# Pooled attention with a two-layer network on one core: the first pair's start in another order, last stores from two engines, query pooling and bound transposes at other places of a pair's fourth step

## The chip, the cores and the metric

One Trainium2 chip, one core. The metric is the device time of one execution in microseconds (us). The kernel before took 812.07 us (median of three runs, 811.73 to 814.13). The engines are named as the profile names them: PE is TensorE (PEld its weight loads), DVE is VectorE, ACT is ScalarE, POOL is GpSimd, SP is SyncE, which here only issues transfers.

## The reference, cut to what matters

```python
# q, k, v: (4, 8, 1152, 64) float32;  batch, heads, rows, head width
q_pool = q.reshape(B, H, S // 2, 2, D).mean(axis=3)
scores = scale * np.matmul(q_pool, k.transpose(0, 1, 3, 2))
attn = np.exp(scores - scores.max(-1)); attn /= attn.sum(-1) + 1e-9
x = np.matmul(attn, v)                        # -> (4, 576, 512), all heads side by side
xn = (x - mean(x)) / np.sqrt(var(x) + 1e-6) * g_ln
out = x + np.maximum(xn @ w_ch1, 0) @ w_ch2   # w_ch1 (512, 2048), w_ch2 (2048, 512)
```

## The kernel before, in words

Two heads of one batch make a *pair*; there are 16 pairs, four to a batch. A pair has 576 pooled query rows per head, cut into 9 tiles of 128 rows (the fifth tile holds 64 rows of each head). One tile is one *step*, so there are 144 steps, and step `i` belongs to pair `i // 9` and has place `j = i % 9` in it. About 20 more steps finish the network. `step(i)` writes out the program; every engine runs its own instructions in just the order in which `step` emits them.

A step's own work: `emit_s` multiplies queries with keys (PE, L372 and L380) into three of the eight banks of `psum`, slot `i % 2`; `emit_max` copies the scores out and finds each row's largest (DVE, L392, "the search" below); `emit_exp` exponentiates (ACT, L399); `emit_hi` and `emit_lo` split the result into two 16-bit halves (ACT L410; DVE L419, or POOL L239 and L417 at places 2, 5 and 8), a transfer transposes them (SP, L422), and four steps later `emit_pv` multiplies with the values (PE, L462) into columns 128 to 257 of the last bank of the slot that holds the next step's scores. In the first 36 steps (batch 0, `on_pe`) TensorE transposes instead (L429) and `emit_pv` works in 32 bits (L453). In those steps the weights are also loaded and split.

From step 36 on each step also runs a *unit* of the two-layer network of a finished batch: 24 matmuls of the first layer (L613), whose result ACT and DVE split into `ht` (L626, L627), or 8 or 12 matmuls of the second (L645), whose end DVE adds into the output (L659).

Operands are scaled by powers of two taken from bounds. For pair `p`, during the steps of pair `p - 1` (queries in part a pair earlier): transfers bring keys and values (`load`, L117, L118, L121) and queries (`load_q`, L129); DVE or POOL adds the two rows that are pooled (`pool_q`, L162), POOL copies the sum (`dup_q`, L166); ACT sums absolute values into `acc` (`bound`, L182). At place 3 `scales_reduce` queues two pieces in `reds`: the first transposes `acc` on PE (L197), after which DVE takes the maximum and writes it on a diagonal (L200 `mx`, L201 `diag`); the second, one step later, multiplies the diagonal with ones on PE (L208), after which `scales` turns the exponent into factors (DVE, L231 `e`, L232 `s`, L234 `sc`). `place()` puts the results of L197 and L208 into columns 258 to 386 of that same last bank. `PREPS` lists the transposes of keys and queries (PE L285, L289, L312, L321) and their splits (ACT L274, L299; DVE L271, L294) at places 4 to 9.

What is read out of `psum` for a step is collected in `evacs` by `until(...)` and written out by `flush()` in the following step, after that step's search, in the order in which it was collected. `bank()` hands out a free bank for a unit or a prep.

Before step 0 the program loads the first tensors, keeps PE running with matmuls on the identity (`warm`, L1048), and goes through bounds, scales, transposes, splits and the first scores of pair 0 one after the other (L1070 to L1100).

Of the kernel before, what the change touches and what calls it, by code (L numbers as in the profile page):

```python
# [24 lines left out]
def tile_pooled_attention_moe(  # L25
# [198 lines left out]
    def scales(p, top, a=0, b=3):  # L224

        st = pair[p]
        e, s, sc = (st[x] for x in ("e", "s", "sc"))
        v = nc.vector
        ei, si = (x.bitcast(I32)[:, a:b] for x in (e, s))
        ti = top.bitcast(I32)  # L230
        v.tensor_scalar(ei, ti, EXPO, None, op0=ALU.bitwise_and)  # L231
        v.tensor_scalar(si, ti, EXPO, EXPO, op0=ALU.bitwise_and, op1=ALU.bitwise_xor)  # L232
        if a == 0:
            v.scalar_tensor_tensor(  # L234
                sc[:, 0:1], e[:, 0:1], -(2.0 ** -6), e[:, 1:2], op0=ALU.mult, op1=ALU.mult
            )
# [69 lines left out]
    def prep_q(p, u):  # L306

        qr, qt, s = raws[p, "q"], qt_of(p), pair[p]["s"]
        ps = bank()
        z = p % HP // 2  # L310
        if u == 2:
            nc.tensor.transpose(ps[:, 0:128], qr[:, C - 1].rearrange("p r d -> p (r d)"), ident)  # L312
            o, n = 512, 128
            hi, lo = (qt[:, a, o:o + n] for a in range(2))
            return split_from((p, "q", u), ps[:, 0:n], s[:, 1:2], hi, lo)

        d = (256, 128)[z]
        rows = ps.rearrange("p (a h n) -> p a h n", h=2, n=d)
        for c in range(4):
            a, n = (0, 64 * c) if z == 0 else (c // 2, 64 * (c % 2))  # L320
            nc.tensor.matmul(  # L321
                out=rows[:, a, :, n:n + 64], lhsT=qr[:, 4 * u + c].rearrange("p r d -> p (r d)"),
                rhs=ident.rearrange("p (h n) -> p h n", h=2), is_transpose=True, start=True, stop=True,
            )
        if z == 0:

            ps = ps.rearrange("p (h n) -> p h n", h=2)
            hi, lo = (
                pair[p]["qt+"][:, 1152 * a:1152 * a + 1280].rearrange("p (h n) -> p h n", h=2)[
                    :, :, 256 * u:256 * u + 256  # L330
                ]
                for a in range(2)
            )
        else:
            hi, lo = (qt[:, a, 640 * u:640 * u + 512] for a in range(2))
        return split_from((p, "q", u), ps, s[:, 1:2], hi, lo)

    PREPS = (
        ((prep_k, 0), (prep_k, 2), (prep_q, 0), (prep_q, 1), (prep_k, 1), (prep_q, 2)),
# [6 lines left out]
    def on_pe(i):  # L346

        return 0 <= i < HP * C
# [248 lines left out]
    def half_of(w, xn, xs, stores, fine=False):  # L597
# [36 lines left out]
        def l2(t, m0, m1):  # L634
# [22 lines left out]
            def evac():  # L657
                x = xs[t]
                nc.vector.scalar_tensor_tensor(  # L659
                    x, ps, inv12[:, w:w + 1], x, op0=ALU.mult, op1=ALU.add  # L660
                )
                if w == 1:
                    for o, dst in stores[t]:
                        nc.sync.dma_start(out=dst, in_=x[o:o + 64])
                    if len(xs) > 1:
                        room["x"] += 1
            return (evac,)
# [135 lines left out]
    for p in range(1, NP):  # L803
# [4 lines left out]
        if p == 1:  # L808
            pre(0, behind_scales)
            pre(i0 + 1, pool_q, p, nc.gpsimd)  # L810
            at(i0 + 1, dup_q, p, nc.gpsimd)
            at(i0 + 2, bound, p, "q")
        elif on_pe(i0):
            at(i0 - 4, load_q, p, (nc.sync,))
            at(i0 - 1, lambda p=p: calm.appendleft((lambda n: pool_q(p, nc.gpsimd), 0)))
            at(i0, lambda p=p: calm.appendleft((lambda n: dup_q(p, nc.gpsimd), 0)))
            at(i0 + 2, bound, p, "q")
        else:
            at(i0 - 8, load_q, p, (nc.sync,))
            at(i0 - 4, pool_q, p, nc.vector)  # L820
            at(i0 - 2, bound, p, "q")
            at(i0 - 1, dup_q, p, nc.gpsimd)
        if not on_pe(p * C):
# [140 lines left out]
    def step(i):  # L964
# [50 lines left out]
        if on_pe(i):  # L1015
            emit_t(i)
            if reds:
                found.append(reds.popleft()())
        elif reds:
            red = reds.popleft()  # L1020
            put = [None]
            until([lambda: put[0]()])
        while turned:
            n, ot = turned.popleft()
            emit_turn(n, ot, i)
        if not on_pe(i):
            if not first:
                a_piece(i)
            if red:
                put[0] = red()  # L1030
            if i in turns:
                a_prep()
            some_units(i)
            if i not in turns:
                a_prep()
        for fn, a in todo.pop(i, ()):
# [13 lines left out]
    with tc.manual_schedule():  # L1050
# [16 lines left out]
        nc.scalar.activation(out=wexp[:, 0:1], in_=nhalf, func=ACTF.Exp)  # L1067
        make_identity(nc, ident)

        warm(110)  # L1070
        st = state(0)
        nc.vector.memset(st["acc"], 0.0)
        pool_q(0, nc.vector)
# [10 lines left out]
            apply_absolute_value=True,  # L1084
        )
        nc.vector.tensor_tensor(st["acc"][:, 0:1], st["acc"][:, 0:1], st["acc"][:, 2:3], op=ALU.max)
        one, two = all_max(st["acc"][:, 0:2], 2, lambda ps: scales(0, ps, 0, 2))
        one()()
        two()()
        free_banks[:] = [6, 7, 3, 4]  # L1090
        parts = [fn(0, u) for fn, u in PREPS[0][:3]]
        for hi, lo in parts:
            hi()
            lo()
        warm(16)
        emit_s(0)
        preps.extend((fn, 0, u) for fn, u in PREPS[0][3:])
        free_banks[:] = [6, 7]
        for h in range(2):
# [34 lines left out]
```

## Time and profile before

| | |
|---|---|
| median of three runs | 812.07 us (811.73 to 814.13) |
| the profiled execution | 812.92 us, of it a span of 811.1 us from the first to the last instruction |
| busy: PE, DVE, ACT, POOL | 783.1, 599.3, 544.4, 341.3 us |
| share of the span on the chain that ended last | PE 67%, POOL 13%, DVE 10%, ACT 3% |

The profile gives for each instruction its start and duration and, where its engine stood idle before it, for how long and what ended the idle time. An engine's idle time costs something only where it is on the chain that ends last; here PE stands idle for only 28 us of 811, so the reading goes by stages and by PE's idle places.

### The profile page before, as it was taken

The page shows a single profiled execution, that of the slowest core. Times are in us where ns is not written, and L with a number is a line of the kernel's source. Part 1 is how long each engine was busy: PE and PEld are TensorE (multiplying, and loading weights), DVE is VectorE, ACT ScalarE, POOL GpSimd, SP SyncE. Part 2 cuts the span into 40 slices and gives each one's busy share as a digit, 9 for nine tenths or more (in the row PEclk, how much of TensorE's full clock was granted, in tenths as well). Part 3 has the DMA queues.
Part 4 walks back from the last instruction along what each step waited for, and adds up shares of the span by engine and source line. Part 5 has one row for each costly group of instructions (what it writes and reads, how often), then busy time and mean ns, then how long its engine had stood idle before and what let it go on. Part 6 is the DMA issues. An engine that isn't in the chain of part 4 may idle for free.

```text
span 811.1 us, 21365 instructions
## 1 busy us (share of the span) xinstructions
PE 783.1 (97%) x8978; PEld 553.7 (68%) x8978; DVE 599.3 (74%) x1174; ACT 544.4 (67%) x788; POOL 341.3 (42%) x338
## 2 busy tenths in 40 slices
PE   8899999989989999989999999999999999999997
PEld 7688888767556666657566666766675757766764
DVE  4599999999989887898777878888787867522121
ACT  3799898877786878787767776787778676211100
POOL 2010243389999963475452524528252423200000
PEclk9999999999999999999999999999999999999999
DMA  5828464208699999998998989896979687401001
GB/s 146 248 68 286 155 195 142 81 17 157 124 192 158 186 162 206 175 191 156 207 167 180 178 176 172 164 198 116 223 136 209 128 146 123 81 1 27 14 1 27
DMA packets 276017, 115.95 MB, mean 143 GB/s; under 512 B 259280, under 2 KB 259280, under 8 KB 275920
## 3 DMA queue, kind: packets, MB, share of 16 engines
q1 hardware_dynamic: 275840, 114.29, 69.9%
q8 instruction: 70, 1.15, 0.6%
q10 hardware_dynamic: 80, 0.29, 0.2%
q14 instruction: 27, 0.22, 0.1%
HBM read 46.14 MB, written 4.72 MB: 63 GB/s over the span
## 4 chain that ended last, share of the span: by engine, by line
PE 67%; POOL 13%; DVE 10%; issue 4%; ACT 3%; DMA 2%; SPq 0%; POOLq 0%; ACTq 0%; DVEq 0%
PE psum L645 19%; PE psum L613 18%; PE psum L372 8%; PE psum L462 7%; PE psum L453 5%; POOL wsl L239 4%; PE psum L429 3%; POOL wsl L786 3%; PE psum L380 2%; POOL hl L417 2%; DVE pe L392 2%; DVE hl L419 1%; DMA vr<-in_v_dram 1%; PE psum L321 1%; PE psum L1048 1%
## 5 line engine op out<-in xcount | busy, mean ns | idle before, releaser
L392 DVE CUSTOM_DVE_ANT_0 pe<-psum,nought,sc 128x1152 f32<-128x1152 f32 x144 | 203.1, 1411 | 17.5 <-PE psum L462 7.5
L399 ACT ACTIVATE pe<-pe,nb 128x1152 f32<-128x1152 f32 x144 | 180.4, 1253 | 31.9 <-DVE nb L392 31.0
L645 PE MATMUL psum<-wsl,ht 128*128 128x512 f16 x864 | 196.6, 379 | 4.7 <-DVE ht L627 3.8
L613 PEld LDWEIGHTS <-wsl 128*128 128x128 f16 x1920 | 169.6, 98 | 20.9 <-issue 3.2
L613 PE MATMUL psum<-xn,wsl 128*128 128x256 f16 x1536 | 176.3, 273 | 2.9 <-DVE xb L659 1.9
L645 PEld LDWEIGHTS <-ht 128*128 128x128 f16 x864 | 81.2, 98 | 93.0 <-issue 5.0
L626 ACT ACTIVATE ht<-psum 128x512 f16<-128x512 f32 x72 | 42.9, 595 | 129.2 <-PE psum L613 129.0
L410 ACT ACTIVATE hl<-pe 128x1152 f16<-128x1152 f32 x108 | 125.6, 1163 | 3.4
L372 PE MATMUL psum<-kt,qt 64*128 64x512 f16 (+1 forms) x960 | 120.2, 382 | 3.1 <-ACT pt L435 2.3
L419 DVE SCALAR_TENSOR_TENSOR hl<-pe,hl 128x1152 f16<-128x1152 f32 x72 | 116.5, 1618 | 0.0
L462 PE MATMUL psum<-vt,pt 128*128 128x65 f16 (+2 forms) x3240 | 106.8, 194 | 0.1
L627 DVE SCALAR_TENSOR_TENSOR ht<-psum,ht 128x512 f16<-128x512 f32 x72 | 49.6, 689 | 74.4 <-ACT ht L626 74.3
L462 PEld LDWEIGHTS <-pt 128*128 128x128 f16 (+1 forms) x3240 | 98.3, 100 | 3.0 <-DMA pt<-hl 0.3
L239 POOL TENSOR_SCALAR pe<-pe 128x1152 f32<-128x1152 f32 x36 | 42.8, 1189 | 119.3 <-ACT hl L410 119.3
L417 POOL TENSOR_TENSOR hl<-pe,hl 128x1152 f16<-128x1152 f32 x36 | 87.1, 2420 | 3.0
L453 PE MATMUL psum<-pt,vt 128*65 128x128 f32 (+1 forms) x720 | 77.4, 263 | 1.2 <-DVE kt L271 1.2
L453 PEld LDWEIGHTS psum<-pt,vt 128*65 128x65 f32 x720 | 71.4, 138 | 1.6 <-DVE kt L271 1.4
L372 PEld LDWEIGHTS <-qt 64*128 64x128 f16 (+1 forms) x960 | 31.6, 96 | 49.5 <-issue 30.8
L380 PEld LDWEIGHTS <-qt 128*128 128x128 f16 (+1 forms) x320 | 17.1, 99 | 63.1 <-issue 63.1
L245 POOL COPY gate<-gate 128x1 f32<-128x1 f32 x27 | 5.0, 184 | 110.7 <-DVE gate L244 110.7
L271 DVE SCALAR_TENSOR_TENSOR qt<-psum,s,qt 128x512 f16<-128x512 f32 (+1 forms) x48 | 29.4, 614 | 29.3 <-ACT qt L274 29.1
L659 DVE SCALAR_TENSOR_TENSOR xb<-psum,inv,xb 128x512 f32<-128x512 f32 x32 | 23.9, 745 | 36.7 <-PE psum L645 36.5
(114 smaller groups left out, 978.3 us busy)
## 6 DMA issues: line engine op xcount, KB each, us to landing
stage<-in_moe_w_ch_dram SPq DMA_DIRECT2D x32, 512.0 KB, 6.9
kr<-in_k_dram SPq DMA_DIRECT2D x16, 576.0 KB, 4.6
vr<-in_v_dram SPq DMA_DIRECT2D x16, 576.0 KB, 5.2
qr<-in_q_dram SPq DMA_DIRECT2D x31, 288.0 KB, 5.1
out_dram<-xb SPq DMA_DIRECT2D x32, 128.0 KB, 2.4
pt<-hl SPq DMA_TRANSPOSE x108, 5.2
kr<-in_k_dram SPq DMA_DIRECT2D x16, 64.0 KB, 4.2
out_dram<-xh SPq DMA_DIRECT2D x4, 128.0 KB, 2.8
```

What stands on the lines that cost most here:

```text
L239: nc.gpsimd.tensor_scalar(dst, src, s, 1.0, op0=ALU.mult, op1=ALU.mult)
L372: nc.tensor.matmul(out=sp[o:o + w, c0:c0 + 512], lhsT=qt[r:r + 64, qa, q0:q0 + w], rhs=kt[r:r + 64, ka, h], start=(a == 0), stop=(a == 2),)
L392: nc.vector.tensor_tensor_reduce(out=st["pe"], in0=st["s"], in1=nought[:, 0:1].to_broadcast([128, S]), scale=pair[i // C]["sc"][:, 0:1], s ...
L399: nc.scalar.activation(out=st["pe"], in_=st["pe"], func=ACTF.Exp, scale=-1.0, bias=st["nb"])
L410: nc.scalar.activation(out=hl[:, 0], in_=st["pe"], func=ACTF.Copy, scale=2.0 ** 15)
L417: nc.gpsimd.tensor_tensor(hl[:, 1], st["pe"], hl[:, 0], op=ALU.subtract)
L419: nc.vector.scalar_tensor_tensor(hl[:, 1], st["pe"], 2.0 ** 15, hl[:, 0], op0=ALU.mult, op1=ALU.subtract)
L453: nc.tensor.matmul(out=ps[0:65, q0:q0 + w], lhsT=vt[:, h, c], rhs=pt[:, 128 * u + q0:128 * u + q0 + w], start=(u == 0), stop=(u == C - 1),)
L462: nc.tensor.matmul(out=dst[:, 0:n], lhsT=pt[:, a + u, q0:q0 + w], rhs=vt[:, h, c, x0:x0 + n], start=(u == 0 and a == 0 and n == 65), stop= ...
L613: nc.tensor.matmul(out=ps[:, o:o + n], lhsT=wsl[:, 8 * w + cc, wa, f * 128:f * 128 + 128], rhs=xn[:, xa * KD + cc, 0:n], start=(m == 0), s ...
L627: lambda: nc.vector.scalar_tensor_tensor(lo, pv, 0.0, hi, op0=ALU.max, op1=ALU.subtract),
L645: nc.tensor.matmul(out=ps, lhsT=hv[0][:, ha, f, t * 128:t * 128 + 128], rhs=wsl[:, 8 * w + 4 + f // 2, wa, (f % 2) * DM:(f % 2) * DM + DM] ...
```

## The change

Five edits, with the names of the functions above.

1. `scales` writes the factor `s` before `e`.
2. Pair 0's start. The warm-up matmuls go from 110 to 84. The transposes of keys (L285, L289) stand ahead of that of `acc`, those of queries right behind it. The first query tiles are split in two halves, one head each (`prep_q_first`); the first scores wait for the first half, and the second half is put among the work of step 0, in bank 7. The second warm-up goes from 16 to 12.
3. `evac` of the second layer: from step 149 on, the second of the two stores of a tile is issued by ACT.
4. For pairs 6 to 15 `load_q` is issued at place 6 of the pair three before (was: place 1 of the pair two before), and `pool_q` stands at place 3 (was: place 5) of the pair two before. `load_q` passes the transposes of its neighbours in SP's queue; nothing else moves there, and POOL's order stays as it was.
5. In steps of place 3 the transpose of `acc` (L197) stands behind the unit, and its reading out behind the unit's.

```diff
@@ scales
+        v.tensor_scalar(si, ti, EXPO, EXPO, op0=ALU.bitwise_and, op1=ALU.bitwise_xor)
         v.tensor_scalar(ei, ti, EXPO, None, op0=ALU.bitwise_and)
-        v.tensor_scalar(si, ti, EXPO, EXPO, op0=ALU.bitwise_and, op1=ALU.bitwise_xor)
...
+    def prep_q_first():
+        qr, s = raws[0, "q"], pair[0]["s"]
+        qt_of(0)
+        ps = bank()
+        rows = ps.rearrange("p (h n) -> p h n", h=2)
+        for c in range(4):
+            nc.tensor.matmul(
+                out=rows[:, :, 64 * c:64 * c + 64], lhsT=qr[:, c].rearrange("p r d -> p (r d)"),
+                rhs=ident.rearrange("p (h n) -> p h n", h=2), is_transpose=True, start=True, stop=True,
+            )
+        x = pair[0]["qt"]
+        parts = []
+        for h in range(2):
+            hi, lo = (x[:, a, 640 * h:640 * h + 256] for a in range(2))
+            parts.append(split_from((0, "q", 0), rows[:, h], s[:, 1:2], hi, lo))
+        return parts
...
-                    for o, dst in stores[t]:
-                        nc.sync.dma_start(out=dst, in_=x[o:o + 64])
+                    for z, (o, dst) in enumerate(stores[t]):
+                        eng = nc.scalar if z and this[0] >= NSTEP + 5 else nc.sync
+                        eng.dma_start(out=dst, in_=x[o:o + 64])
...
-            at(i0 - 8, load_q, p, (nc.sync,))
-            at(i0 - 4, pool_q, p, nc.vector)
+            early_q = not on_pe(i0 - 6)
+            at(i0 - (12 if early_q else 8), load_q, p, (nc.sync,))
+            at(i0 - (6 if early_q else 4), pool_q, p, nc.vector)
...
-            until([lambda: put[0]()])
+            behind = i % C == 3
+            if not behind:
+                until([lambda: put[0]()])
...
-            if red:
+            if red and not behind:
                 put[0] = red()
             if i in turns:
                 a_prep()
             some_units(i)
+            if red and behind:
+                until([red()])
...
-        warm(110)
+        warm(84)
...
+        free_banks[:] = [4, 6, 3, 7]
         one, two = all_max(st["acc"][:, 0:2], 2, lambda ps: scales(0, ps, 0, 2))
-        one()()
+        (k_hi, k_lo), (k8_hi, k8_lo) = (prep_k(0, u) for u in (0, 2))
+        found_top = one()
+        q_parts = prep_q_first()
+        found_top()
         two()()
-        free_banks[:] = [6, 7, 3, 4]
-        parts = [fn(0, u) for fn, u in PREPS[0][:3]]
-        for hi, lo in parts:
-            hi()
-            lo()
-        warm(16)
+        warm(12, psum[:, 0])
+        k_hi()
+        q_parts[0][0]()
+        k8_hi()
+        k_lo()
+        q_parts[0][1]()
+        k8_lo()
         emit_s(0)
+        waiting.clear()
+        until(q_parts[1], 7)
+        waiting.add(7)
```

What this does to the engines' order is shown at three places. Line numbers of the changed kernel are its own: L1074 there is L1048 here, L345 the transposes of `prep_q_first`, L390 and L398 are L372 and L380, L410 is L392, L437 is L419, L480 is L462, L528 and L529 are L510 and L511, L631 is L613, L645 is L627.

PE before, behind the warm-up at the start (`acc` holds the bounds, `kr` and `qr` the raw keys and queries):

```order
L1048 MATMUL psum<-ident 128x128
L197 MATMUL psum<-ident,acc 2x128
L208 LDWEIGHTS ones
L208 MATMUL psum<-diag,ones 128x2
L285 MATMUL psum<-ident,kr 128x128 x4
L289 MATMUL psum<-ident,kr 128x128 x2
L321 MATMUL psum<-ident,qr 128x2x64 x4
```

The same place in the changed kernel:

```order
L1074 MATMUL psum<-ident 128x128
L285 MATMUL psum<-ident,kr 128x128 x4
L289 MATMUL psum<-ident,kr 128x128 x2
L197 MATMUL psum<-ident,acc 2x128
L345 MATMUL psum<-ident,qr 128x2x64 x4
L208 LDWEIGHTS ones
L208 MATMUL psum<-diag,ones 128x2
```

The ten transposes that stood behind the two bound matmuls now stand ahead of and between them.

PE before in the step of place 3 of pair 9, around the transpose of `acc` (`pt` and `vt` are the multiplication with values, `wsl` the first of the unit's 24 matmuls):

```order
L462 LDWEIGHTS pt
L462 MATMUL psum<-vt,pt 128x65
L197 MATMUL psum<-ident,acc 3x128
L613 LDWEIGHTS wsl
L613 MATMUL psum<-xn,wsl 128x256
```

The same place in the changed kernel, where `wsl` is the last of the unit's 24 matmuls and `qt` the next step's scores:

```order
L631 LDWEIGHTS wsl
L631 MATMUL psum<-xn,wsl 128x256
L197 MATMUL psum<-ident,acc 3x128
L390 LDWEIGHTS qt
L390 MATMUL psum<-kt,qt 128x512
```

L197 moved from the front of the unit to its back.

DVE before, from the unit's split at the end of place 3 to the half `lo` in place 4 of the same pair:

```order
L627 SCALAR_TENSOR_TENSOR ht<-psum,ht 128x512
L392 ISA pe,nb<-psum,nought,sc 128x1152
L392 ISA nb 128x1
L200 TENSOR_REDUCE mx3<-psum 3x1
L201 SCALAR_TENSOR_TENSOR diag<-psum,mx3,ident 3x3
L510 TENSOR_SCALAR r<-psum,s 128x1
L511 RECIPROCAL r<-r 128x1
L627 SCALAR_TENSOR_TENSOR ht<-psum,ht 128x512
L419 SCALAR_TENSOR_TENSOR hl<-pe,hl 128x1152
```

And in the changed kernel:

```order
L645 SCALAR_TENSOR_TENSOR ht<-psum,ht 128x512
L162 TENSOR_TENSOR qr<-qr 128x9x64
L410 ISA pe,nb<-psum,nought,sc 128x1152
L410 ISA nb 128x1
L528 TENSOR_SCALAR r<-psum,s 128x1
L529 RECIPROCAL r<-r 128x1
L645 SCALAR_TENSOR_TENSOR ht<-psum,ht 128x512
L200 TENSOR_REDUCE mx3<-psum 3x1
L201 SCALAR_TENSOR_TENSOR diag<-psum,mx3,ident 3x3
L437 SCALAR_TENSOR_TENSOR hl<-pe,hl 128x1152
```

The pooling L162 stands ahead of the search, and `mx` and `diag` moved from right behind the search to behind the split of the next unit.

## Rows read from the trace of the kernel before

**Rows 1.** Busy time by stretch: PE, PEld, DVE, ACT, POOL, clock, DMA share, GB/s

```profile
25.70:27.00 1.30, 1.04 (x5) 0.37 (x5) 0.00 (x0) 1.30 (x2) 0.00 (x0) 0.67 0.93 225
180.00:290.00 110.00, 101.73 (x1265) 69.43 (x1264) 99.07 (x164) 83.08 (x113) 103.97 (x74) 1.00 0.92 164
400.00:500.00 100.00, 99.02 (x1261) 67.18 (x1259) 78.97 (x148) 75.37 (x105) 38.72 (x32) 1.00 1.00 180
```

**Rows 2.** Timeline of the start: start, us, engine, line, op, operands [idle before]

```profile
8.53 0.16 DVE L1086 TENSOR_TENSOR acc<-acc 128x1 f32<-128x1 f32 x1
9.54 0.27 PE L197 MATMUL psum<-ident,acc 128*2 128x128 f32 x1
...
10.50 0.16 PE L208 MATMUL psum<-diag,ones 128*128 128x2 bf16 x1 [0.69 <-DVE diag L201]
...
10.70 0.16 DVE L231 TENSOR_SCALAR e<-psum 128x2 int32<-128x2 int32 x1 [0.25 <-PE psum L208]
...
11.24 0.69 ACT L274 ACTIVATE kt<-psum,s 128x512 f16<-128x512 f32 x1 [2.87 <-PE psum L285]
...
11.96 0.75 DVE L271 SCALAR_TENSOR_TENSOR kt<-psum,s,kt 128x512 f16<-128x512 f32 x1 [0.91 <-ACT kt L274]
...
12.75 0.49 DVE L294 SCALAR_TENSOR_TENSOR kt<-psum,s,kt 64x256 f16<-64x256 f32 x1
...
14.40 0.28 PE L380 MATMUL psum<-kt,qt 128*128 128x128 f16 x2
...
14.52 1.06 PE L1048 MATMUL psum<-ident 128*128 128x128 f16 x16
14.72 1.42 DVE L392 CUSTOM_DVE_ANT_0 pe<-psum,nought,sc 128x1152 f32<-128x1152 f32 x1 [0.70 <-PE psum L380]
...
15.42 0.61 PE L321 MATMUL psum<-ident,qr 128*128 128x128 f32 x4
...
17.50 1.20 PE L429 MATMUL psum<-ident,pe 128*128 128x128 f32 x9 [0.50 <-ACT pe L399]
...
20.11 0.37 SPq L117 DMA_DIRECT2D kr<-in_k_dram  x1
...
23.96 1.16 ACT L182 ACTIVATE kt<-kr 128x1152 f16<-128x1152 f32 x1 [1.96 <-DMA kr<-in_k_dram]
```

**Rows 3.** Timeline of PE in places 3 and 4 of pair 9

```profile
406.91 0.27 PE L197 MATMUL psum<-ident,acc 128*3 128x128 f32 x1
...
409.74 0.82 PE L372 MATMUL psum<-kt,qt 64*128 64x512 f16 x6
...
411.43 0.17 PE L208 MATMUL psum<-diag,ones 128*128 128x3 bf16 x1
```

**Rows 4.** Timeline of DVE from place 4 to place 6 of pair 9

```profile
407.22 1.42 DVE L392 CUSTOM_DVE_ANT_0 pe<-psum,nought,sc 128x1152 f32<-128x1152 f32 x1 [0.71 <-PE psum L197]
...
408.57 0.28 DVE L200 TENSOR_REDUCE mx<-psum 3x1 f32<-3x129 f32 x1
408.88 0.21 DVE L201 SCALAR_TENSOR_TENSOR diag<-psum,mx,ident 3x3 bf16<-3x3 f32 x1
...
419.68 1.41 DVE L392 CUSTOM_DVE_ANT_0 pe<-psum,nought,sc 128x1152 f32<-128x1152 f32 x1
...
421.34 0.67 DVE L627 SCALAR_TENSOR_TENSOR ht<-psum,ht 128x512 f16<-128x512 f32 x1
```

**Rows 5.** Timeline of PE at its idle places after pooling, pairs 7, 9 and 12

```profile
336.18 2.75 PE L645 MATMUL psum<-wsl,ht 128*128 128x512 f16 x12 [0.66 <-DVE ht L627]
...
422.07 2.10 PE L645 MATMUL psum<-wsl,ht 128*128 128x512 f16 x9 [0.98 <-DVE ht L627]
...
551.51 0.66 PE L321 MATMUL psum<-ident,qr 128*128 128x128 f32 x4 [0.27 <-DVE kt L294]
```

**Rows 6.** Timeline of POOL, values of pair 6 scaled during pair 5

```profile
246.59 0.74 POOL L239 TENSOR_SCALAR vt<-vr,s 128x576 f16<-128x576 f32 x1 [0.52 <-DVE s L232]
```

**Rows 7.** Timeline of the end: the last two stores

```profile
807.29 1.11 SPq L664 DMA_DIRECT2D out_dram<-xb  x2
```

## The prediction, made before the changed kernel ran

> **What bounds the kernel now.** I read the chain of waits first, then busy time by stretch, then the timelines at the few places where TensorE stands idle. The stretches [rows 1] show two regimes. From 180 to 290 us GpSimd is busy for 103.97 of 110 us and TensorE idles for 8.3 of them: GpSimd's queue of weight splits sets the pace, and a wait of TensorE there costs nothing by itself. From 400 to 500 TensorE is busy for 99.02 of 100 us, and the 0.98 us that are missing are one row, a unit of pair 9 that waits for VectorE behind the pooling [rows 5]. So from about 290 us on each microsecond in which TensorE waits is one at the end, and there is almost no other idle time in which a new wait could be hidden. The two ends of the kernel are chains of their own.
>
> **The start.** Before, the bounds' transpose L197 at 9.54 stands directly behind the warm-up, though VectorE has the bounds ready at 8.69 [rows 2]. 26 warm-up matmuls at 0.056 (16 from 14.52 to 15.42, [rows 2]) are 1.46 less; six key transposes, at the 0.13 of the nine in row 17.50, put back 0.8: L197 at 8.9. The path from L197 to L208 takes 0.96 and from there to the first factor 0.20 + 0.16, so `s`, which now comes first, is there at 10.2, and ScalarE, no longer waiting for key transposes, begins its first split about 1.0 earlier than 11.24. From there: 0.72 to VectorE's low part of the keys, 0.75 for it, then 0.49 for half the queries and 0.49 for the last keys (the L294 row) with some 0.04 between them, in place of 0.75 for all queries; L380 at 12.8, and 0.32 later the search of step 0, at 13.1 instead of 14.72. That is −1.6.
>
> Not all of it lasts. The second half of the queries sits in bank 7, and the next query transposes (L321) take that bank. VectorE reads it only behind the search: 13.1 + 1.35 + 0.49, so L321 starts at 15.0 instead of 15.42. From L321 to the issue of the next keys' load TensorE worked 4.69, 0.50 of it the idle time at 17.50, which goes; the load is issued at 19.2 instead of 20.11. ScalarE waits for its landing for 1.96 us before L182 [rows 2], and TensorE behind it, so the start is worth what this load gains, **−0.9** (0 to −1.6).
>
> **Place 3: the transpose behind the unit.** Here is the step that decides. In place 4 the search had to wait 0.71 us for L197 [rows 4], although it doesn't read what L197 writes: L197's columns lie in the same bank as the scores that the search reads, and the row shows that the search isn't let go until L197 is done. L197 now stands behind the unit, so the search is held until the unit is through. Replay of pair 9: L197 and the unit only trade places on TensorE, so the next scores stay at 409.74 [rows 3] and L197 starts some 0.13 ahead, at 409.6. The search follows by the 0.31 between 406.91 and 407.22, at 409.9 instead of 407.22. VectorE then does, in the order of the changed kernel, the search and the two short instructions on `r` (1.66 from a search to the unit's split, 419.68 to 421.34), the split (0.67), `mx` (0.31 to the next) and `diag` (0.21) [rows 4]: done at 412.8. TensorE reaches L208, which reads `diag`, at 411.43 [rows 3] and stands in order: the unit, the next key transposes and scores are queued behind it. That is a wait of 1.4, or **1.35** with the few hundredths by which VectorE's instructions overlap. Before, `diag` was ready at 409.1 and the wait was zero.
>
> The same holds in pairs 7 to 13, seven times 1.35 or 9.45. In pair 14 place 4 has no split on VectorE, so 0.67 less: 0.7. Together **+10.1** (bounds: 0.15 a pair, if the search weren't held and only `mx` stood later, so 1.1; and 1.6 a pair, if the pooling beside GpSimd's work also held the search, so 12).
>
> **What goes.** The pooling leaves place 5, where it made the search of place 6 and the unit's split late, and TensorE with them: 0.66 in pair 7, 0.98 in pair 9, 0.27 in pair 12 [rows 5]. With pair 8 (0.37 and, for L197 waiting on ScalarE's bound, 0.80) and pair 11 these are six idle places of 3.87 in all: **−3.9**. All six go, since after the new wait VectorE reaches place 6 earlier against TensorE than before. In place 3 the pooling costs nothing: it ends long before the search may start at 409.9. The query load, moved in SP's queue, meets fewer transposes' landings that TensorE needs soon; at zero.
>
> **Pairs 4 to 6**, under GpSimd's pace: the new waits fall into time that TensorE loses anyway. But GpSimd waited in pair 5 for VectorE's factor by 0.52 [rows 6], and that factor comes later by some 0.3: **+0.3** (0 to +4, three waits of 1.35).
>
> **The end.** The last two stores are issued one after the other by SP, 1.11 for both [rows 7]. With the second on ScalarE, idle there, one issue goes: **−0.55**. [...]
>
> **Sum**: −0.9 + 10.1 − 3.9 + 0.3 − 0.55 = **+5.05 us** on the profiled execution's 812.92, so 817.97. That execution lay 0.85 above the median of the three runs, 812.07; so I predict a median of **817.1**.
>
> **The rivals.**
> *The search isn't held (the other side).* If the wait in row 407.22 is put down to L197 by the order of ends and it is really the multiplication with values ahead of it, the search stays near 407.3, and `diag` is ready about 0.15 after L208's turn. Then seven times 0.15 stand against −3.9: 812.07 − 0.9 + 1.05 − 3.9 − 0.55 = 807.8. It decides at the first place 3: the search starts before or after the unit ends. Against it: the 0.71 ends at 407.22, just behind L197's end at 407.18. Chance 0.08.
> *The wait is there but is made up again.* VectorE has 1.7 us less to do in place 5 and could let TensorE run closer later. Half of the 10.1 regained gives 812.1. Against it: between 400 and 500 us TensorE has nothing left to regain. Chance 0.14.
> *Pairs 4 to 6 pay too and the start gives nothing*: 817.1 + 3.75 + 0.9, about 821.8. Chance 0.10.
> *The clock falls after the new waits.* [...] Chance 0.06.
> The forecast keeps 0.62.
>
> **How the numbers follow.** About 0.3%, 2.4 us, is what a measurement of this kernel can tell from no change: below 809.6 is faster, above 814.5 slower. Faster takes the first rival and a little of the second: 0.10. The same: most of the second: 0.15. Slower: the forecast, the last two and the rest, 0.75. The range from 811.5 to 820.0 holds the forecast with its bounds, nearly all of the second rival and parts of the last two, about 0.8; it leaves out the first rival and the far ends.
>
> **What would show it.** In the changed kernel's timeline: the search of step 0 near 13.1 and the next keys' load at 19.2; in pair 9 the search of place 4 behind L197, and L208 with some 1.35 us of idle time, ended by VectorE's `diag`, in each of pairs 7 to 13; no idle time of TensorE behind the pooling; the wait of the search for L197 some 2 us per pair in the table of waits, where VectorE lost 0.7. I am wrong if L208 has no idle time, or if it has it and TensorE's total idle time behind 290 us doesn't grow by some 6 us.

## The result and the profile after

The changed kernel takes 817.55 us (median of six runs, 816.95 to 819.44), the kernel before 813.37 in the runs beside it (six, 811.73 to 814.18). The ratio is 1.0055, with a 95% interval of 1.0041 to 1.0070: slower, by 0.4 to 0.7%. The profiled execution took 818.19 us with a span of 816.4, 5.3 more than before. The forecast was a median of 817.1, and +5.05 on the profiled execution.

The waits at L208 come first. In the changed kernel TensorE stood idle before this line as the view of one source line says (cause, us in all, times):

```profile
its engine sat idle before it (us, times) until:
  DVE diag L201: 12.2, 12
```

Before it was 0.7 us, once, at the start [rows 2]. Eleven of the twelve are pairs 4 to 14, one each. Pair 9, TensorE (start, us, engine, line, op, operands, idle time before it), against [rows 3]:

```profile
408.72 2.78 PE L631 MATMUL psum<-xn,wsl 128*128 128x256 f16 x24
411.33 0.27 PE L197 MATMUL psum<-ident,acc 128*3 128x128 f32 x1
411.54 0.82 PE L390 MATMUL psum<-kt,qt 64*128 64x512 f16 x6
...
414.47 0.16 PE L208 MATMUL psum<-diag,ones 128*128 128x3 bf16 x1 [1.08 <-DVE diag L201]
```

VectorE beside it, against [rows 4]. The pooling L162 is done in time, the search of place 4 waits for L197 and starts 0.32 after it, and `diag` comes last in a row of search, r, split, `mx` and `diag`:

```profile
409.56 0.75 DVE L162 TENSOR_TENSOR qr<-qr 128x576 f32<-128x576 f32 x1
411.65 1.42 DVE L410 CUSTOM_DVE_ANT_0 pe<-psum,nought,sc 128x1152 f32<-128x1152 f32 x1 [1.34 <-PE psum L197]
...
413.32 0.67 DVE L645 SCALAR_TENSOR_TENSOR ht<-psum,ht 128x512 f16<-128x512 f32 x1
413.91 0.27 DVE L200 TENSOR_REDUCE mx<-psum 3x1 f32<-3x129 f32 x1
414.21 0.21 DVE L201 SCALAR_TENSOR_TENSOR diag<-psum,mx,ident 3x3 bf16<-3x3 f32 x1
```

The six idle places behind the pooling [rows 5] are gone, all of them. Busy time by stretch (columns as in [rows 1]):

```profile
25.00:27.00 2.00, 1.40 (x8) 0.41 (x7) 0.00 (x0) 2.00 (x4) 0.00 (x0) 1.00 0.93 285
28.00:30.00 2.00, 2.00 (x11) 2.00 (x10) 0.96 (x2) 1.56 (x3) 0.00 (x0) 0.50 1.02 397
...
287.00:290.00 3.00, 3.00 (x17) 2.07 (x15) 2.81 (x8) 0.57 (x2) 0.60 (x1) 0.50 0.28 54
...
400.00:500.00 100.00, 97.84 (x1251) 66.44 (x1250) 76.86 (x138) 74.79 (x106) 37.89 (x31) 1.00 1.00 182
```

From 400 to 500 us TensorE is busy for 97.84 where it was 99.02: two waits at L208 of 1.08 each stand where one of 0.98 stood. Two stretches at the granted clock of 0.50 stand out, at 28 and at 287 us. The second lies in pair 6. VectorE, GpSimd and TensorE there:

```profile
280.56 2.38 POOL L435 TENSOR_TENSOR hl<-pe,hl 128x1152 f16<-128x1152 f32 x1
...
281.38 2.17 DVE L162 TENSOR_TENSOR qr<-qr 128x576 f32<-128x576 f32 x1
283.48 1.41 DVE L410 CUSTOM_DVE_ANT_0 pe<-psum,nought,sc 128x1152 f32<-128x1152 f32 x1
...
286.29 0.16 PE L208 MATMUL psum<-diag,ones 128*128 128x3 bf16 x1 [1.88 <-DVE diag L201]
286.32 4.45 PE L631 MATMUL psum<-xn,wsl 128*128 128x256 f16 x24
```

Here the pooling takes 2.17 us beside GpSimd's L435, not 0.75, and delays the search beyond L197; the wait at L208 becomes 1.88, and behind it the clock falls: the unit's 24 matmuls take 4.45 us, not 2.78. Beside L435 the pooling takes 2.17 us in pair 5 too and 2.29 in pair 8; in pairs 7 and 9, where GpSimd is idle, it takes 0.75.

The start, against [rows 2]:

```profile
13.59 1.42 DVE L410 CUSTOM_DVE_ANT_0 pe<-psum,nought,sc 128x1152 f32<-128x1152 f32 x1 [0.36 <-PE psum L398]
...
15.47 0.66 PE L321 MATMUL psum<-ident,qr 128*128 128x128 f32 x4 [1.02 <-DVE qt L271]
...
19.49 0.37 SPq L117 DMA_DIRECT2D kr<-in_k_dram  x1
...
23.51 1.16 ACT L182 ACTIVATE kt<-kr 128x1152 f16<-128x1152 f32 x1 [2.64 <-DMA kr<-in_k_dram]
...
25.28 0.37 PE L390 MATMUL psum<-kt,qt 64*128 64x512 f16 x1 [2.73 <-ACT pt L453]
...
27.04 1.75 PE L447 MATMUL psum<-ident,pe 128*128 128x128 f32 x9
...
28.58 3.29 PE L471 MATMUL psum<-pt,vt 128*65 128x128 f32 x18
```

The search of step 0 is 1.13 earlier, the keys' load 0.62, TensorE's restart behind the wait 0.46; but the wait is 2.73 us long (2.06 before), and the low clock behind it now falls on L447 and L471, by which TensorE itself sets the pace. From TensorE's restart to the start of pair 1 it takes 30.06 us here (25.28 to 55.34) and 29.54 before (25.74 to 55.28); in e3 and e6 below, where the clock doesn't fall, it takes 28.39 (with the new start 28.38 in e9, e10 and e12 and 27.79 in e8). So the fall costs 1.67 us here and cost 1.15 before, and the 0.46 is gone: pair 1 starts at 55.34 us, before at 55.28. The end, against [rows 7]:

```profile
812.88 0.50 ACTq L684 DMA_DIRECT2D out_dram<-xb  x1
812.91 0.47 SPq L684 DMA_DIRECT2D out_dram<-xb  x1
```

From the start of VectorE's last addition to the end of the span it is 4.30 us now, 4.62 before.

### The profile page after: what moved, and what is told of

It is laid out like the page before. It is cut to its first block, busy times and chain, and to the rows that moved or that the text cites. A ratio compares the mean times of both kernels' runs of the same rounds, so it can differ in the third digit from the quotient of the medians.

```text
span 816.4 us, 21303 instructions
## 1 busy us (share of the span) xinstructions
PE 784.2 (96%) x8948; PEld 554.6 (68%) x8948; DVE 599.4 (73%) x1175; ACT 545.1 (67%) x789; POOL 340.8 (42%) x338
## 3 DMA queue, kind: packets, MB, share of 16 engines
q8 instruction: 70, 1.15, 0.6%
## 4 chain that ended last, share of the span: by engine, by line
PE 77%; DVE 13%; ACT 4%; DMA 2%; issue 2%; POOL 1%; SPq 0%; ACTq 0%; POOLq 0%; DVEq 0%
PE psum L631 21%; PE psum L663 20%; PE psum L390 9%; PE psum L480 8%; PE psum L471 6%; DVE pe L410 4%; PE psum L447 3%; PE psum L398 3%; DVE hl L437 2%; PE psum L321 2%; PE psum L285 1%; DMA stage<-in_moe_w_ch_dram 1%; DVE qr L162 1%; PE psum L1074 1%; ACT pe L417 1%
## 5 line engine op out<-in xcount | busy, mean ns | idle before, releaser
L410 DVE CUSTOM_DVE_ANT_0 pe<-psum,nought,sc 128x1152 f32<-128x1152 f32 x144 | 202.9, 1409 | 25.9 <-PE psum L197 13.8
L417 ACT ACTIVATE pe<-pe,nb 128x1152 f32<-128x1152 f32 x144 | 180.4, 1253 | 32.1 <-DVE nb L410 31.3
L631 PEld LDWEIGHTS <-wsl 128*128 128x128 f16 x1920 | 169.8, 98 | 29.9 <-issue 11.4
L631 PE MATMUL psum<-xn,wsl 128*128 128x256 f16 x1536 | 178.0, 274 | 2.8 <-DVE xb L677 2.0
L390 PE MATMUL psum<-kt,qt 64*128 64x512 f16 (+1 forms) x960 | 119.7, 380 | 3.8 <-ACT pt L453 3.0
L437 DVE SCALAR_TENSOR_TENSOR hl<-pe,hl 128x1152 f16<-128x1152 f32 x72 | 115.4, 1603 | 0.0
L480 PE MATMUL psum<-vt,pt 128*128 128x65 f16 (+2 forms) x3240 | 106.8, 193 | 0.0
L645 DVE SCALAR_TENSOR_TENSOR ht<-psum,ht 128x512 f16<-128x512 f32 x72 | 49.4, 687 | 72.8 <-ACT ht L644 72.8
L480 PEld LDWEIGHTS <-pt 128*128 128x128 f16 (+1 forms) x3240 | 98.4, 100 | 2.6 <-issue 0.2
L435 POOL TENSOR_TENSOR hl<-pe,hl 128x1152 f16<-128x1152 f32 x36 | 85.6, 2379 | 3.0
L471 PE MATMUL psum<-pt,vt 128*65 128x128 f32 (+1 forms) x720 | 78.6, 265 | 1.2 <-DVE kt L271 1.2
L471 PEld LDWEIGHTS psum<-pt,vt 128*65 128x65 f32 x720 | 72.7, 140 | 1.6 <-DVE kt L271 1.4
L390 PEld LDWEIGHTS <-qt 64*128 64x128 f16 (+1 forms) x960 | 31.6, 96 | 50.1 <-issue 31.8
L398 PEld LDWEIGHTS <-qt 128*128 128x128 f16 (+1 forms) x320 | 17.4, 99 | 63.1 <-issue 62.8
L271 DVE SCALAR_TENSOR_TENSOR qt<-psum,s,qt 128x512 f16<-128x512 f32 (+2 forms) x49 | 29.7, 605 | 30.7 <-ACT qt L274 30.5
```

Source lines behind the costliest of these rows:

```text
L390: nc.tensor.matmul(out=sp[o:o + w, c0:c0 + 512], lhsT=qt[r:r + 64, qa, q0:q0 + w], rhs=kt[r:r + 64, ka, h], start=(a == 0), stop=(a == 2),)
L410: nc.vector.tensor_tensor_reduce(out=st["pe"], in0=st["s"], in1=nought[:, 0:1].to_broadcast([128, S]), scale=pair[i // C]["sc"][:, 0:1], s ...
L417: nc.scalar.activation(out=st["pe"], in_=st["pe"], func=ACTF.Exp, scale=-1.0, bias=st["nb"])
L435: nc.gpsimd.tensor_tensor(hl[:, 1], st["pe"], hl[:, 0], op=ALU.subtract)
L437: nc.vector.scalar_tensor_tensor(hl[:, 1], st["pe"], 2.0 ** 15, hl[:, 0], op0=ALU.mult, op1=ALU.subtract)
L471: nc.tensor.matmul(out=ps[0:65, q0:q0 + w], lhsT=vt[:, h, c], rhs=pt[:, 128 * u + q0:128 * u + q0 + w], start=(u == 0), stop=(u == C - 1),)
```

## The experiments

Twelve more kernels ran in three groups, each group beside runs of the kernel before (medians 814.27, 813.77 and 813.77). The table gives the start of the search of step 0 and of the first search of pairs 1, 5, 7 and 9 in the traces, in us from the span's start, and the median time:

| kernel | step 0 | pair 1 | pair 5 | pair 7 | pair 9 | median |
|---|---|---|---|---|---|---|
| before | 14.72 | 55.28 | 221.96 | 306.18 | 389.96 | 813.4 to 814.3 |
| changed | 13.59 | 55.34 | 222.06 | 308.15 | 391.75 | 817.55 |
| e1, changed without edit 5 | 13.60 | 55.20 | 221.84 | 305.45 | 388.06 | 809.46 |
| e5, start alone | 13.15 | 54.53 | 221.35 | 305.77 | 390.25 | 813.39 |
| e6, before with the wait filled | 13.99 | 53.50 | 220.24 | 304.64 | 390.58 | 815.27 |
| e8, e1 with the wait filled | 12.87 | 52.80 | 220.28 | 307.56 | 394.15 | 815.27 |
| e9, changed with the wait filled | 13.01 | 53.31 | 219.92 | 307.03 | 393.47 | 818.36 |

### Edit 5 taken away (e1)

```diff
-            behind = i % C == 3
-            if not behind:
-                until([lambda: put[0]()])
+            until([lambda: put[0]()])
...
-            if red and not behind:
+            if red:
                 put[0] = red()
...
-            if red and behind:
-                until([red()])
```

> The changed kernel without edit 5: L197 stands at the front of place 3's unit again; edits 1 to 4 stay. Theory A (the waits at L208 and the clock behind the longest of them are the whole loss, the moved pooling is a gain): L208 has no idle time in pairs 7 to 14 (7.45 us less) and pair 6's unit takes 2.78 us again instead of 4.45 (about 1.6 less); the six idle places behind the pooling stay away, since it is the pooling that made them. Time of before -3.9 -0.3 for the end, so about 4 us under before. Rival B (the idle places went because TensorE now waits earlier, not because the pooling moved): they come back, and the time is that of before within 0.5 us. Rival C (the loss comes from the start or from the pooling in place 3): the time stays above before.

809.46 us (809.10 to 810.72), 0.9940 of before, interval 0.9925 to 0.9955: 4.8 us under before. The view of line L208, and one stretch (columns as in [rows 1]):

```profile
  DVE diag L201: 0.5, 2
```

```profile
400.00:500.00 100.00, 100.00 (x1285) 68.08 (x1282) 79.86 (x146) 76.67 (x106) 40.18 (x34) 1.00 1.00 179
```

Theory A holds. The waits at L208 are gone from pair 6 on (0.26 is left in pair 5), pair 6 keeps its clock, and between 400 and 500 us TensorE never waits, so the idle places left because the pooling moved (B is out). What is left are waits of L197 for ScalarE's bound of the values, 2.7 us in five pairs (2.1 in three in the kernel before); one of them in TensorE's timeline:

```profile
280.19 0.27 PE L197 MATMUL psum<-ident,acc 128*3 128x128 f32 x1 [0.68 <-ACT kt L182]
```

### The pooling alone (e2)

```diff
-            at(i0 - 8, load_q, p, (nc.sync,))
-            at(i0 - 4, pool_q, p, nc.vector)
+            early_q = not on_pe(i0 - 6)
+            at(i0 - (12 if early_q else 8), load_q, p, (nc.sync,))
+            at(i0 - (6 if early_q else 4), pool_q, p, nc.vector)
```

> The kernel before with edit 4 alone: queries are loaded earlier and pooled in place 3. Theory A: the idle places of TensorE at 336, 380, 422, 465, 507 and 551 us (3.87 in all) are gone, nothing new appears, 3.5 to 4 us under before; in pair 9 the pooling fills the 0.71 us that the search of place 4 waited for L197. Rival B: at least 2 of the 3.87 us come back at other places, and the time is within 2 us of before. Rival D (the pooling beside the search of place 4 makes L208 wait): idle time at L208 of 0.1 to 0.7 a pair.

821.15 us (815.14 to 824.25), 1.0077 of before, interval 1.0058 to 1.0097. None of the three had this: B's "at least 2 us come back at other places" did come, but at L197, and the time is 6.9 us over before. The idle places behind the pooling are gone, but L197 waits in five pairs for the bound of the values, 7.3 us in all (2.1 before), and VectorE has nothing to do with it. Pair 7, ScalarE and TensorE:

```profile
320.74 1.16 ACT L182 ACTIVATE kt<-vr 128x1152 f16<-128x1152 f32 x1 [3.21 <-DMA vr<-in_v_dram]
...
322.05 0.38 PE L197 MATMUL psum<-ident,acc 128*3 128x128 f32 x1 [2.62 <-ACT kt L182]
```

The same place in the kernel before:

```profile
319.54 1.17 ACT L182 ACTIVATE kt<-vr 128x1152 f16<-128x1152 f32 x1 [1.25 <-DMA vr<-in_v_dram]
...
321.02 0.27 PE L197 MATMUL psum<-ident,acc 128*3 128x128 f32 x1
```

The values land later against the work, and at the front of the unit L197 has to wait for them. The clock fell beside this wait (nine of the unit's matmuls took 2.13 us behind it, all 24 took 2.78 in the unit before), and behind one more of 2.97 us in pair 5. And the profiled execution was the fastest of ten, 6 us under the median: its mean granted clock was 0.996, that of the others 0.988 to 0.994. So the others lost more to the clock; where they did, no trace shows.

### The transpose behind the unit alone (e3)

```diff
+            behind = i % C == 3
+            if not behind:
                 until([lambda: put[0]()])
...
+            if red and behind:
+                until([red()])
```

> The kernel before with edit 5 alone: L197 behind the unit of place 3, pooling still in place 5. Theory A (the terms add up): the L208 waits of 7.45 us in pairs 7 to 14, about 1.6 for the clock in pair 6, and the six idle places of 3.87 stay at least in part, since the pooling is still ahead of the search of place 6: 6 to 9.5 us over before. Rival B (the waits alone clear the idle places): L208 waits as in the changed kernel, no idle place behind the pooling, about 5.5 us over before with the start and the end as they were.

822.99 us (821.78 to 825.70), 1.0115 of before, interval 1.0089 to 1.0140: 8.7 us over, within A's range: the two terms add up, though A's 1.6 us for the clock in pair 6 have no part in it, since the clock stayed at 1.00 throughout in this trace. Against executions of before that kept it too (810.8 to 811.7, see e6) this one, 821.78, is some 10 us over. TensorE has the wait at L208 and still the one behind the pooling in place 5, which the first doesn't clear:

```profile
412.99 0.16 PE L208 MATMUL psum<-diag,ones 128*128 128x3 bf16 x1 [1.08 <-DVE diag L201]
...
423.85 2.75 PE L645 MATMUL psum<-wsl,ht 128*128 128x512 f16 x12 [1.21 <-DVE ht L627]
```

In this kernel, too, L208 waits 1.08 in pair 9, and L197 never for the values: behind the unit it is late enough.

### Read out first (e4)

```diff
             if red and behind:
-                until([red()])
+                evacs.insert(0, (None, red()))
```

> The changed kernel, with only VectorE's order changed: the maximum and the diagonal of the bounds (L200, L201) are read out first of all behind the search of place 4, ahead of r and of the unit's split. L197 stays behind the unit, and the search of place 4 is still held by it. Theory A (what costs is the time from the held search to the diagonal): 0.21 + 0.16 + 0.67 us less on that path, so L208 waits 0.1 or less in place of 1.08 in most pairs; in pairs 8 and 12, where the unit's bank must be free of the split some instructions later, about 0.5 is left; in pair 6 less wait and no lower clock. 6 to 8 us under the changed kernel, 1 to 3 us under before. Rival E (the late search and with it the late scores are the loss, and L208 only shows it first): the wait moves to the next instruction that VectorE or ScalarE feeds, and the time stays within 1.5 us of the changed kernel.

811.41 us (810.20 to 812.07), 0.9960 of before, interval 0.9944 to 0.9975: 2.9 us under before, 6 to 8 under the changed kernel. Only VectorE's order differs. Pair 9, VectorE and TensorE:

```profile
407.54 1.42 DVE L410 CUSTOM_DVE_ANT_0 pe<-psum,nought,sc 128x1152 f32<-128x1152 f32 x1 [1.38 <-PE psum L197]
...
409.45 0.16 PE L208 MATMUL psum<-diag,ones 128*128 128x3 bf16 x1 [0.17 <-DVE diag L201]
```

The search is held as long as in the changed kernel, 1.38 us by L197, and yet nearly all of the loss is gone (E is out). What cost the time is the row from the held search to `diag`, in front of L208.

### Another bank (e7)

```diff
-            u = this[0] if on_pe(this[0]) else pv_slot[0]
+            u = this[0] if on_pe(this[0]) or this[0] % C == 3 else pv_slot[0]
```

> The changed kernel with every engine's order as it is, but in place 3 the transposed bounds are put into the last bank of the other slot of scores, which the search of place 4 doesn't read. Theory H (the search is held because L197 writes into the bank that it reads): in pair 9 the search follows the pooling directly, some 1.3 us ahead of L197's end, without idle time for L197, and TensorE's idle time at L208 is gone; as VectorE then waits for ScalarE's half of the unit, the diagonal is ready some 0.4 us earlier, and the wait goes to the values of place 4 (L480), which write into the new bank while the bounds are unread: 0.6 to 0.9 a pair there; 1 to 3 us under the changed kernel. Rival (the search waits for the unit or for TensorE's queue, not for the bank): the search stays where it was, behind L197, and L208 keeps 1.08.

819.15 us (818.11 to 820.96), 1.0056 of before, interval 1.0036 to 1.0077. The orders of all engines are those of the changed kernel. Pair 9, VectorE and TensorE:

```profile
410.44 1.41 DVE L410 CUSTOM_DVE_ANT_0 pe<-psum,nought,sc 128x1152 f32<-128x1152 f32 x1
...
413.58 0.98 PE L480 MATMUL psum<-vt,pt 128*128 128x65 f16 x27 [0.62 <-DVE diag L201]
414.40 0.17 PE L208 MATMUL psum<-diag,ones 128*128 128x3 bf16 x1
```

The search follows the pooling at once, 1.28 us ahead of L197 (411.72), and L208 has no wait; what holds the search in the changed kernel is the bank, as the prediction had it. The time didn't follow: the wait moved to L480, which writes into the new bank, and L197 itself now waits in four pairs (0.43 to 1.01 us) for ScalarE's reading of it. Only the mechanism of H holds, not its price.

### The start alone (e5)

The diff is that of `scales`, `prep_q_first` and the start in the change.

> The kernel before with edits 1 and 2 alone, the new start. As predicted first: search of step 0 at 13.1 to 13.6, keys' load at 19.2 to 19.5, the whole 0.9 kept, so pair 1 starts 0.9 us earlier than before. [...] If the clock doesn't fall in the profiled execution, pair 1 starts 2.3 to 2.7 us earlier than in the trace of before.

813.39 us (812.13 to 814.81), 0.9990 of before, interval 0.9972 to 1.0008: no difference. The first search is at 13.15, as the prediction had it, pair 1 starts 0.75 earlier than in the trace of before; by pair 9 that is lost (390.25 against 389.96). The gain is there and is given back, and not to the clock alone: the fall takes a part ahead of pair 1, the rest goes between pairs 1 and 9.

### The wait for keys filled, in the kernel before (e6)

```diff
             if i < 3:
-                warm(16, bank())
+                warm(50 if i == 2 else 16, bank())
```

> The kernel before, with 50 warm-up matmuls instead of 16 in the step where TensorE waits for the next pair's keys, so that it stands idle for some 0.2 us there instead of 2.06. Theory F (the clock falls because of the wait, and this alone costs the time that four TensorE groups are longer by: 0.64 + 0.11 + 0.76 + 0.16 = 1.7 us): granted clock 1.00 from 25 to 31 us, pair 1 starts 1.7 us earlier, the time 1 to 1.8 us under before (a part, since the clock need not fall in every execution). Rival G (the clock falls anyway, because of the power drawn or of the loads at that time, or the extra matmuls only delay the next ones): granted clock 0.5 to 0.7 somewhere from 25 to 31 us as before, and the time within 0.5 us of before or over it.

815.27 us (814.21 to 818.78), 1.0022 of before, interval 1.0000 to 1.0044. The stretches, and ScalarE and TensorE in pair 7:

```profile
25.00:27.00 2.00, 1.53 (x9) 0.55 (x9) 0.00 (x0) 2.00 (x5) 0.00 (x0) 1.00 0.99 244
27.00:31.00 4.00, 4.00 (x44) 3.23 (x43) 1.68 (x3) 3.92 (x8) 0.00 (x0) 1.00 1.00 384
318.00:319.00 1.00, 1.00 (x27) 0.50 (x18) 0.00 (x0) 0.00 (x0) 1.00 (x1) 1.00 0.03 3
```

```profile
319.80 1.16 ACT L182 ACTIVATE kt<-vr 128x1152 f16<-128x1152 f32 x1 [3.05 <-DMA vr<-in_v_dram]
...
321.11 0.27 PE L197 MATMUL psum<-ident,acc 128*3 128x128 f32 x1 [1.46 <-ACT kt L182]
```

The clock stays at 1.00 and pair 1 starts 1.78 earlier, as Theory F says; pair 7 is still 1.54 ahead. Then L197 waits for the values, here and in four other pairs (5.4 us in all, 2.1 before), and pair 9 is 0.62 behind. With no edit of the change in it, this kernel loses at the same place as e2.

But an earlier start alone doesn't bring these waits. In e3 pair 1 starts as early (53.55, here 53.50), and there the same load is issued at 313.46 us, here at 313.22. From issue to landing, in e3 and in e6:

```profile
vr<-in_v_dram SPq DMA_DIRECT2D x1, 576.0 KB, 4.4
```

```profile
vr<-in_v_dram SPq DMA_DIRECT2D x1, 576.0 KB, 6.6
```

Nor is an earlier start always lost. In the trace of before the clock's fall at the start is the only one, and the mean granted clock is 0.998. Of 65 executions of the kernel before beside the experiments 34 have this mean and a median of 813.5 us; five have 1.000, so that they can't have that fall, and take 810.8 to 811.7. These five keep some 2 us to the end. Three of e6 have 1.000 as well and take 814.2 to 815.0. What the filling itself changes no run shows.

### The wait filled in the changed kernel and in others (e8 to e12)

In all of them `warm(16, bank())` becomes `warm(60 if i == 2 else 16, bank())`, except in e11. e8 is e1 with it, e9 the changed kernel, e10 the kernel of e4. e11 is the kernel of e4 with

```diff
-            behind = i % C == 3
+            behind = i % C == 3 and i // C in (5, 6, 7, 8, 13)
```

and e12 is e11 with the filling.

> Edits 1 to 4 without edit 5, and 60 warm-up matmuls instead of 16 where TensorE waits for the next pair's keys. Theory F: no fall of the clock behind that wait, L447 1.2 and L471 2.0 us there again, pair 1 starts about 1.9 us earlier than in the same kernel without the filling; some 807.5 to 808.5, 5.5 to 6.5 us under before. Rival G: 809 to 810, as without the filling.

> The changed kernel, with 60 warm-up matmuls instead of 16 where TensorE waits for the next pair's keys. Theory F (in the changed kernel the start's gain is given back to the clock alone; behind the unit L197 never waits for the bound of the values, so an earlier start can be kept): granted clock 1.00 from 25 to 31 us, pair 1 starts some 2.4 us ahead of before, pair 9 is 1.5 to 2.4 us earlier than in the changed kernel without the filling, and the time 1.5 to 2.5 us under it. Rival K (an earlier start is lost in pairs 4 to 8 in any case, since the loads of keys and values don't come earlier with it): pair 9 starts where it did, and the time is within 0.7 us of the changed kernel.

> The run in which the bounds are read out first behind the search of place 4, with the same filling at the start. Theory F: 1.3 to 2 us under that run (811.4), so 809.4 to 810.1, and no L197 waits for ScalarE's bound L182 in pairs 5 to 8. Rival K: 811 to 812, with the gain gone by pair 9.

> The bounds' transpose stands behind the unit, and its result is read out first behind the search, only in the steps of pairs 5 to 8 and 13, where L197 at the front of the unit waited for the bound of the values (0.54, 0.68, 0.21, 0.37 and 0.88 us in the run without edit 5); elsewhere it stands at the front as before. Theory: the L197 waits of 2.7 us go, L208 waits of 0.83 and 0.65 come in pairs 5 and 6, and the rest of the pairs lose nothing; 808.0 to 809.5. Rival K: 809.5 to 811, the gain of the one lost at the next load.

> The same with the filling at the start. Theory F: the earlier start of 1.3 to 1.9 us is kept through pairs 5 to 8; 806.5 to 808, the fastest of all. Rival K: within 0.7 us of the same kernel without the filling.

e8: 815.27 us (812.92 to 818.04), 1.0014 of before, interval 0.9995 to 1.0033. e9: 818.36 (815.69 to 820.27), 1.0062, 1.0038 to 1.0086. e10: 812.89 (811.11 to 815.51), 0.9996, 0.9980 to 1.0011. e11: 809.70 (809.29 to 810.52), 0.9959, 0.9944 to 0.9975. e12: 809.77 (807.51 to 811.77), 0.9953, 0.9936 to 0.9971.

Theory F failed in each that was filled. In e12 rival K came; e9 and e10 are a little worse than K (e9 0.8 us over the changed kernel, its pair 9 1.7 us later). e8 lies far over both its theories: it differs from e1 by 44 matmuls in a wait, starts pair 1 2.4 us earlier and is 5.8 us slower. e11 lies in K's range: the waits of L197 are gone, and it is no faster than e1. In the changed kernel I had held L197 to be covered, and it is; but ScalarE's queue isn't. Pair 6 of e9:

```profile
279.92 1.16 ACT L182 ACTIVATE kt<-vr 128x1152 f16<-128x1152 f32 x1 [4.00 <-DMA vr<-in_v_dram]
...
284.25 0.27 PE L398 MATMUL psum<-kt,qt 128*128 128x128 f16 x2 [2.00 <-ACT xb L540]
```

ScalarE waits 4.00 us for the values, everything queued behind is late, and TensorE waits for a reading of `psum` there. Behind it the clock fell once more (0.50 from 285 to 287 us). e10 and e12 have the same wait of 2.00 us at the same place. The load itself took longer: in pairs 5 and 6 the values needed 6.5 to 6.9 us in all four filled kernels, 4.8 to 4.9 in e1, e4 and e11. The transfer of the values in pair 6 from issue to landing (KB, us), in e1 and in e8:

```profile
vr<-in_v_dram SPq DMA_DIRECT2D x1, 576.0 KB, 4.9
```

```profile
vr<-in_v_dram SPq DMA_DIRECT2D x1, 576.0 KB, 6.7
```

e1, e11 and e12 are the fastest, within 0.3 us of each other; they beat both kernels, and nothing that was added to e1 did better.

## Why the prediction came out as it did

The sum was forecast as +5.05 and measured as +5.3 on the span. That they lie so close is luck: errors of both signs cancelled.

| term | forecast | measured |
|---|---|---|
| start, at pair 5 | -0.9 | +0.1 |
| L208, pairs 7 to 14 | +10.1 | +7.45 |
| six idle places | -3.9 | -3.9 |
| pairs 4 to 6 | +0.3 | +1.9 |
| end | -0.55 | -0.3 |

The wait at L208 came out 2.65 us short; the start, which gave 1.0 less than forecast, and pairs 4 to 6, which cost 1.6 more, made up for it. By one of its own signs the prediction was wrong: TensorE's idle time behind 290 us was to grow by some 6 us. From the first search of pair 7 to the end the two kernels have, before and changed (columns as in [rows 1]):

```profile
306.18:811.10 504.92, 494.98 (x5853) 333.53 (x5850) 336.92 (x623) 304.43 (x430) 175.90 (x171) 1.00 0.74 136
308.15:816.40 508.25, 495.00 (x5853) 333.84 (x5850) 340.64 (x623) 305.08 (x430) 175.94 (x171) 1.00 0.72 134
```

TensorE's work is the same, and its idle time grows by 3.3 us, from 9.9 to 13.3 (counted from 290 us it is 2.3). The other 2 of the 5.3 us were lost ahead of pair 7, mostly in pair 6.

**The wait at L208** was the step that decides, and its mechanism is right: e7 shows the bank, e4 the row on VectorE, e1 the whole. Its size is off. In pair 9 the row from the search to the end of `diag` took 2.77 us (411.65 to 414.42) for the 2.9 forecast, and TensorE needed 2.06 from L197 to its turn at L208 (411.33 to 413.39), not 1.83, so it waited 1.08 where 1.35 was forecast. The search waited 1.34 for L197, not some 2. Pair 13 waited 0.60, pair 14 0.48 for 0.7. The upper bound, a pooling beside GpSimd that holds the search itself, came true in pairs 5 and 6 (1.86 and 1.88).

**The six idle places** went as said. Five went for the reason given: they stay in e3, where the pooling stays, and are gone in e1, where L208 doesn't wait. The sixth, the 0.80 in pair 8, was L197 waiting for the bound; there it is edit 5 that covers it, and e1 still has 0.37 of it.

**The query load "at zero"** is the term that the runs leave least certain. Edit 4 alone (e2) is 6.9 us over before, with 7.3 us of waits for the values where there were 2.1. Beside edits 1 to 3 (e1), with L197 at the front of the unit as well, these waits are 2.7 and the kernel is 4.8 under before. So the price isn't zero in every kernel; but that edit 4 makes the waits isn't shown, since e6, without it, has 5.4. In the changed kernel L197 comes late enough to be free of them (1.49 us of ScalarE's waiting in pair 7 reach no one), so it couldn't show them. The early pair 1 of e2's trace (53.46, the clock didn't fall there) isn't enough to explain it either, as e3 has the same and its values land in time. What sets e2 apart from e1 stays open.

**The start** gained 1.0 rather than 1.6 at the first search, if one takes all traces: 12.87 to 13.60 in ten with the new start, 13.99 to 14.72 in four with the old, so the row 14.72 was a late one. The load's 0.62 came close to the 0.9. What I didn't price is the longer wait behind it, 2.73 us, and the fall of the clock on work that TensorE is bound by: 0.55 for L447 and 1.2 for L471 against their 1.20 and 2.13 in e6. All six traces with the new start and an unfilled wait (2.52 to 2.77 us) have the fall, and pair 1 starts at 54.53 to 55.34 in them; the changed kernel's is the latest. Traces without that fall start pair 1 at 53.46 to 53.55 with the old start and at 52.80 to 53.31 with the new, where the wait is filled: some 0.45 us, the worth of the edit there. In e5 and e9 nothing of it is left by pair 9.

**Pairs 4 to 6**: 1.61 of the 1.9 is lost in pair 6, where the unit behind the wait took 1.67 longer: the rival "the clock falls after the new waits", which came true behind one of eleven waits.

**The end** gave 0.3 of 0.55: both stores are issued within 0.03 us, but ScalarE's took 2.7 us to land where SP's second took 2.3 before. The nine traces with edit 3 have 4.27 to 4.34 us from the start of the last addition to the end, the five without it 4.62 to 4.87.

**Left open**: why the values land up to 2 us later in some kernels. In e6 the DMA engines move 3 GB/s from 318 to 319 us with that load unfinished. The gap itself isn't new: in the kernel before they move 7 GB/s from 320.5 to 321.5 us, in e3 7 GB/s from 319 to 320, but there the values had landed 1.0 and 1.1 us before it. So in these traces the load is late where the gap meets it. An addition of GpSimd (L417) starts with the gap in e6 (317.94) and 1 us ahead of it in the other two; in e12 a like gap (3 GB/s from 278 to 279 us) lies beside another of its instructions. What opens the gap, and why it meets the load in the filled kernels, no run took apart.

## What to carry over

A wait that is moved behind longer work is free only if everything that the receiving engine has queued between still ends before the next reader's turn: list that row, and put the short read-outs at its front (e4 got back 6 to 8 us by order alone). Price edits together and not one by one: edit 4 alone ended 6.9 us later (e2), and beside edits 1 to 3 it ended 4.8 earlier (e1). And a microsecond saved at the start isn't yet one at the end: e8 saved 2.4 there and ended 5.8 later, while five executions of the kernel before kept some 2.

## What the hardware showed that I had not expected

The clock falls behind some waits and not behind others of the same length. In the changed kernel it fell behind the 1.88 us in pair 6 and not behind the 1.86 in pair 5. Behind the wait for keys, 2.06 us, it fell in the kernel before [rows 1]; in e3, with the same start and the same wait, it didn't, and pair 1 starts 1.73 us earlier:

```profile
25.16 0.37 PE L372 MATMUL psum<-kt,qt 64*128 64x512 f16 x1 [2.06 <-ACT pt L435]
```

```profile
27.00:31.00 4.00, 4.00 (x43) 3.24 (x43) 1.69 (x3) 3.92 (x8) 0.00 (x0) 1.00 1.00 349
```

At the start one and the same kernel differs from execution to execution: of 65 of the kernel before 34 have the mean clock of the trace with the fall, 0.998, and five have 1.000, which leaves no room for it. For the later waits the traces show more order: in five kernels (changed, e8, e9, e10, e12) the clock fell to 0.50 behind the wait in pair 6, of 1.88 to 2.45 us, and in the changed kernel, e10 and e12 it stayed at 1.00 behind that in pair 5, of 1.86, 1.95 and 1.90. What makes the difference no run took apart. A wait near 2 us was thus worth its length, or its length and up to some 1.7 us more (1.15 at the start of the kernel before, 1.67 in pair 6 of the changed one).

And a value load of one size took 4.4 us in e3 and 6.6 in e6, though issued at nearly the same time, 313.46 and 313.22 us.
